# One load queue, a logarithm for the first two standard deviations, and moved copies in a fused attention and feed-forward kernel

## The chip, the cores and the metric

The kernel runs on one core of one Trainium2 chip. A core has five engines that run on their own and wait for each other by semaphores: TensorE (PE in the profile; its weight loads are listed apart as PEld), VectorE (DVE), ScalarE (ACT), GpSimd (POOL), and SyncE (SP), which here only issues DMA transfers. Each engine works through its own list of instructions in order: an instruction that waits holds up all behind it on the same engine, and nothing on the others unless they need its result. The metric is device time in microseconds (us); less is better. The median of three runs before the change is 281.26 us (281.19 to 281.33).

## What is computed

A transformer block on x of 2048 rows by 640 columns, in bf16: linear attention with 32 heads of 20 columns, then a gated feed-forward of width 1536. Cut to what matters:

```python
qkv = layernorm(x) @ wqkv                      # q, k, v per head, head width 20
pq, pk = q @ w_phi[h], k @ w_phi[h]
phi_q = concat(softmax(pq), softmax(-pq));  phi_k = concat(softmax(pk), softmax(-pk))
kv = sum_s phi_k[s] (x) v[s];  z = sum_s phi_k[s]
o  = (phi_q @ kv) / (phi_q . z + 1e-6)
h  = x + o @ wo
y  = layernorm(h)
out = h + (gelu(y @ w_gate) * (y @ w_up)) @ w_down
```

A layernorm here is (x - mean) / sqrt(var + 1e-5) with no weights. The q-by-w_phi and k-by-w_phi products are folded into the weights once: Wk2 = W_k times a block-diagonal of w_phi, likewise Wq2.

## The kernel before, in words

The 2048 rows are 16 tiles t = 0..15 of 128 rows, four tiles to a block b = 0..3 (`x_sb[b]`). The order of the work on every engine is the order of the program text (a manual schedule); no planner moves anything.

**Loads** (lines 160 to 178). The first row tile (`x_sb[0][:,0]`), tiles 2 and 3, then W_v in three pieces, tiles 4 and 5, W_k by a transposing DMA (`WkT`), tiles 8 to 11, W_q transposed (`WqT`), tiles 12 to 15 are issued from SyncE in that order; tile 1, `wphi` and tiles 6 and 7 are issued from ScalarE. ScalarE loads its table for `Exp` by a first small activation (line 168).

**Start** (lines 345 to 377). Ten matmuls on zeros keep TensorE busy. For each of tiles 0 to 3: `ln_st` takes the mean and variance with two `bn_stats` over 320 columns and one `bn_aggr` on VectorE (lines 106, 110), then 1/std on GpSimd by an addition and a power of -0.5 (lines 112, 114); `ln_ap` applies it on VectorE (line 130, tile `ln`); `ln_tp` transposes on TensorE into a PSUM tile `tp` (line 138) and copies it into `LN1T` (line 139). An argument `between` puts another operation after the first of the two `bn_stats`. `v_part` and `v_tile` are the products with W_v (`pv`), evacuated by ScalarE to `vS` (line 271). `BD`, the block-diagonal of w_phi, is one VectorE operation (line 356). `fold` (lines 201 to 226) forms W_k times BD in five pieces d = 0..4 (`wa`), each copied from PSUM by ScalarE for even d and by VectorE for odd d. PSUM tiles come from one pool of four double banks (`psG`), so a product can start only when the tile that used its bank has been evacuated.

**K loop** (lines 382 to 421), t = 0..15: product with Wk2 (`pk`), two `Exp` on ScalarE (`E`, line 283), V product and evacuation for tile t+4, layernorm applied for tile t+6 and transposed by DMA, row sums (`sk`, line 290), reciprocals and scaling of V (`vt`, line 298), and the accumulation `kvp`. At t = `T3` the PSUM pool is closed and reopened with three tiles and the accumulator. At t = 4..8 (`FQ`) one piece of W_q is folded.

**Q and attention for the first tiles** (lines 610 to 643): products with Wq2 (`pq`), two `Exp` each (`Eq`, line 343), and attention of tiles 0 and 1.

**Feed-forward** (lines 656 to 665). `weave(units, stages)` runs a list of units, `gate_up` (a gate and an up product, `gu`, then Gelu on ScalarE and a product on VectorE) and `down` (`pd`, 12 matmuls for each half of 640 columns), and puts each stage of a later tile's attention in front of the unit whose index it names; a stage whose index is past the last unit is kept for the next `weave`. The eight stages of a tile are `attn_a` (`ab`), `attn_b`, `attn_b2`, `attn_b3`, `attn_c` (product `po` with W_o), `attn_d` (VectorE: residual and row sum), `attn_d2` (ScalarE: squares; GpSimd: five small operations to 1/std) and `attn_e` (ScalarE: layernorm; DMA transpose into `LN2T`). With `SHORT2 = (0, 2, 3, 4, 10, 10, 11, 13)` and start index i, `attn_c` of the tile is at i + 10 and `attn_e` at i + 13. The second `weave` has 16 units: 12 `gate_up` for columns 256 to 511 of block 0, then four `down`. The third starts with `gate_up` of block 1, which reads `LN2T` of tiles 4 to 7 whole. The last `down` of the kernel is done in two halves, each added to the residual (`y`, line 575) and stored.

Of the kernel before, what the change touches and what calls it, by code (L numbers as in the profile page):

```python
# [9 lines left out]
F32 = mybir.dt.float32  # L10
# [7 lines left out]
def kernel(  # L18
# [12 lines left out]
    nc = tc.nc  # L31
# [12 lines left out]

    H0 = [(P * c) // Dh for c in range(NC)]
    NH = [(P * c + P - 1) // Dh - H0[c] + 1 for c in range(NC)]
    NWARM = 10
    VP = (0, 2, 4, 6, 9, 11)
    FQ = (4, 5, 6, 7, 8)

    QG = ((0, 1), (2, 3), (4, 5), (6,), (7, 8), (9, 10), (11, 12), (13, 14), (15,), (16, 17), (18, 19))
    QT = (15, 15, 15, 15)
    WA, WB = 2,0
    T3 = 3
    VC = Dh + 1
    KC = Dh + 2

# [26 lines left out]
    kmask = const.tile([P, NC, 4], BF16, name="kmask")  # L84
    BD = const.tile([P, NC, 8, Dh], BF16, name="BD")
    nhalf = const.tile([P, 2], F32, name="nhalf")

    def eq(t, c, s):
        for E, g in zip(Eq, QG):
# [6 lines left out]
    def gtile(name):  # L96
        return psG.tile([P, 2, 512], F32, name=name, tag="G")

    def ln_stats(pool, tiles, tag, act=True, between=None):

        n = len(tiles)
        mv = small(pool, [P, n, nc.vector.BN_AGGR_DIM], "mv" + tag)
        stats = small(pool, [P, n, 2, nc.vector.BN_STATS_DIM], "stats" + tag)
        for j, xt in enumerate(tiles):
            for i in range(2):
                nc.vector.bn_stats(stats[:, j, i, :], xt[:, i * HD:(i + 1) * HD])  # L106
                if between and i == j == 0:
                    between()
        for j in range(n):
            nc.vector.bn_aggr(mv[:, j, :], stats[:, j])  # L110
        ve = small(pool, [P, n], "ve" + tag)
        nc.gpsimd.tensor_scalar_add(ve, mv[:, :, 1], EPS)
        rstd = small(pool, [P, n], "rstd" + tag)
        nc.gpsimd.tensor_tensor(rstd, ve, nhalf[:, 0:n], op=ALU.pow)  # L114

        mr = small(pool, [P, n], "mr" + tag)
        if act:
            for j in range(n):
                nc.gpsimd.tensor_scalar(mr[:, j:j + 1], mv[:, j, 0:1], rstd[:, j:j + 1], -1.0,
                                        op0=ALU.mult, op1=ALU.mult)  # L120
        return [(xt, mv[:, j, 0:1], rstd[:, j:j + 1], mr[:, j:j + 1]) for j, xt in enumerate(tiles)]
# [11 lines left out]
    def transpose_to(dst, src, on_pe, on_dve=False):  # L133

        if on_pe:
            tp = psG.tile([P, 16, P], BF16, name="tp", tag="G")
            for c in range(NC):
                nc.tensor.transpose(tp[:, c, :], src[:, c * P:(c + 1) * P], ident)
            (nc.vector.tensor_copy if on_dve else nc.scalar.copy)(dst, tp[:, 0:NC, :])  # L139
        else:  # L140
            nc.sync.dma_start_transpose(dst, src)

# [15 lines left out]


    nc.gpsimd.memset(nhalf, -0.5)  # L160
    nc.sync.dma_start(x_sb[0][:, 0:1, :], x_v[:, 0:1, :])
    nc.scalar.dma_start(x_sb[0][:, 1:2, :], x_v[:, 1:2, :])
    nc.sync.dma_start(x_sb[0][:, 2:4, :], x_v[:, 2:4, :])
    for c0, c1 in ((0, 2), (2, 4), (4, 5)):
        nc.sync.dma_start(Wv[:, c0:c1, :], w_v[:, c0:c1, 2 * D:3 * D])

    ones = fp.tile([P, 2], F32, name="ones")
    nc.scalar.activation(ones, nhalf, ACTF.Exp)
    nc.scalar.dma_start(wphi, phi_v.rearrange("(c p) f -> p c f", p=P))
    nc.sync.dma_start(x_sb[1][:, 0:2, :], x_v[:, 4:6, :])  # L170
    nc.scalar.dma_start(x_sb[1][:, 2:4, :], x_v[:, 6:8, :])
    nc.sync.dma_start_transpose(WkT, A_wqkv[:, D:2 * D])
    wo_v = A_wo.rearrange("(c p) n -> p c n", p=P)
    wg_v = B_w_gate.rearrange("(c p) n -> p c n", p=P)
    wu_v = B_w_up.rearrange("(c p) n -> p c n", p=P)
# [25 lines left out]
    def fold(WT, W2, halves, ds=range(NC)):  # L201


        runs = []
        for c in range(NC):
            lo, hi = H0[c] * Dh, (H0[c] + NH[c]) * Dh
            for u in range(2):
                a, b = max(lo, u * HD), min(hi, (u + 1) * HD)
                if a < b:
                    runs.append((u, c, a, b))  # L210
        runs.sort()
        for d in ds:
            wa = gtile("wa")
            for i, (u, c, a, b) in enumerate(runs):
                nc.tensor.matmul(wa[:, u, a - u * HD:b - u * HD], lhsT=WT[:, c, d * P:(d + 1) * P],  # L215
                                 rhs=BD[:, c].rearrange("p a b -> p (a b)")[:, a - H0[c] * Dh:b - H0[c] * Dh],
                                 start=(i == 0 or runs[i - 1][0] != u),
                                 stop=(i + 1 == len(runs) or runs[i + 1][0] != u), skip_group_check=True)
            dst, src = W2[:, d, :].rearrange("p (u f) -> p u f", u=2), wa[:, :, 0:HD]
            if halves:  # L220
                dst = W2[:, d, :].rearrange("p (c u f) -> p u c f", c=NC, u=2)
                src = src.rearrange("p u (c f) -> p u c f", c=NC)
            if d % 2 == 0:
                nc.scalar.copy(dst, src)
            else:
                nc.vector.tensor_copy(dst, src)

    lnp, Ek, Vt = {}, {}, {}

    def ln_st(*tiles, act=True, between=None):  # L230
        for t, v in zip(tiles, ln_stats(p1, [x_sb[t // 4][:, t % 4, :] for t in tiles], "1", act, between)):
            lnp[t] = v

    def ln_ap(t, on_act=False, on_pe=False):
        ln = (ln_act if on_act else ln_dve)(p1, "1", *lnp[t])
        if on_pe:
            lnp[t] = ln
        else:
            transpose_to(LN1T[t // 4][:, :, t % 4 * P:(t % 4 + 1) * P], ln, False)

    def ln_tp(t, on_dve=False):
        transpose_to(LN1T[t // 4][:, :, t % 4 * P:(t % 4 + 1) * P], lnp[t], True, on_dve)
# [98 lines left out]
    def q_exp(j, signs=(0, 1)):  # L341
        for s in signs:
            nc.scalar.activation(Eq[j][:, :, s, :], pqs[j][:, 0:len(QG[j])], ACTF.Exp, scale=(1.0, -1.0)[s])  # L343

    ln_st(0, act=False)
    ln_st(1, act=False)
    ln_ap(0, on_pe=True)
    ln_tp(0)
    warm(WA)
    ln_st(2, act=False, between=lambda: ln_ap(1, on_pe=True))  # L350
    ln_tp(1)
    warm(WB)
    ln_st(3, act=False)
    ln_ap(2, on_pe=True)

    nc.vector.tensor_tensor(BD, wphi[:, :, None, :].to_broadcast([P, NC, 8, Dh]),
                            hmask[:, :, :, None].to_broadcast([P, NC, 8, Dh]), ALU.mult)
    ln_ap(3, on_pe=True)
    v_part(0, 0, 1, 2, 3, 4)
    v_part(1, 0, 1)  # L360
    ln_tp(2)
    v_part(1, 2, 3, 4)
    ln_tp(3)
    v_ev(0)
# [175 lines left out]
    def attn_ln(t, on_pe=False):  # L540
        st[t] = (ln_dve if on_pe else ln_act)(p2, "2", *st[t])
# [20 lines left out]
    def down(b, tl, u):  # L562
        if u == 0:
            st["pd"] = gtile("pd"), p2.tile([P, D], BF16, name="y", bufs=4)
        pd, y = st["pd"]
        if u == 1 and b == NB - 1 and tl == 3:
            pd = gtile("pd")
        for f in range(NF):
            nc.tensor.matmul(pd[:, u, 0:HD], lhsT=st[b, "g", f][:, tl * P:(tl + 1) * P],  # L569
                             rhs=Wd[:, f, u * HD:(u + 1) * HD],  # L570
                             start=(f == 0), stop=(f == NF - 1))
        last = b == NB - 1 and tl == 3
        if u == 1 or last:
            a = u if last else 0
            nc.vector.tensor_tensor(y.rearrange("p (u f) -> p u f", u=2)[:, a:u + 1], pd[:, a:u + 1, 0:HD],  # L575
                                    x_sb[b][:, tl, :].rearrange("p (u f) -> p u f", u=2)[:, a:u + 1], ALU.add)
            stores.append((lag, o_v[:, 4 * b + tl, a * HD:(u + 1) * HD], y[:, a * HD:(u + 1) * HD]))
            if b == NB - 1 and tl >= 2:
                store(lag)
# [23 lines left out]
    def gus(b, a0, a1):  # L603
        return [(gate_up, b, f, a0, a1) for f in range(NF)]
# [33 lines left out]
    attn_e(0, True, True)  # L638
    q_mm(q + 6)
    q_exp(q + 6)  # L640
    attn_ln(1, True)
    attn_e(1, True, True)
    attn_a(2, 2)
# [2 lines left out]
    def attn_at(t, i, offs):  # L646
# [9 lines left out]
    weave(gus(0, 0, 256) + downs(0, (0, 1)),  # L656
          attn_at(2, 0, (-1, 0, 1, 2, 7, 7, 8, 10)) + attn_at(3, 1, SHORT) + attn_at(4, 6, SHORT2) + attn_at(5, 9, SHORT2) +
          attn_at(6, 13, SHORT2))
    weave(gus(0, 256, 512) + downs(0, (2, 3)), attn_at(7, 1, SHORT2))
    for b in range(1, NB):  # L660
        stages = []
        if b + 1 < NB:
# [34 lines left out]
```

The softmax here doesn't subtract the row's maximum and nothing guards it: scores larger than these inputs give would overflow.

## Time and profile before

| What | Value |
|---|---|
| median of 3 runs | 281.26 us |
| span of the profiled execution | 279.4 us |
| TensorE busy | 271.9 us, 97% |
| VectorE, ScalarE, GpSimd busy | 166.0, 139.9, 96.5 us |
| granted TensorE clock | 1.00 |

The profile gives, for each engine, how long it was busy; then rows of instructions grouped by source line and operands; and the chain of work that ended last, followed back from the last instruction to what released it each time. A share of busy time is an average over stages with different limits: in the 10 us from 20 to 30 us VectorE is busy 9.75 us and ScalarE 8.79 us, in the 20 us from 240 to 260 us 6.55 and 5.58 us. A busy TensorE is not one at its peak, since the ends of pipelined matmuls are modelled.

### The profile page before, as it was taken

The page shows a single profiled execution, that of the slowest core. Times are in us where ns is not written, and L with a number is a line of the kernel's source. Part 1 is how long each engine was busy: PE and PEld are TensorE (multiplying, and loading weights), DVE is VectorE, ACT ScalarE, POOL GpSimd, SP SyncE. Part 2 cuts the span into 40 slices and gives each one's busy share as a digit, 9 for nine tenths or more (in the row PEclk, how much of TensorE's full clock was granted, in tenths as well). Part 3 has the DMA queues.
Part 4 walks back from the last instruction along what each step waited for, and adds up shares of the span by engine and source line. Part 5 has one row for each costly group of instructions (what it writes and reads, how often), then busy time and mean ns, then how long its engine had stood idle before and what let it go on. Part 6 is the DMA issues. An engine that isn't in the chain of part 4 may idle for free.

```text
span 279.4 us, 5750 instructions
## 1 busy us (share of the span) xinstructions
PE 271.9 (97%) x2326; PEld 171.5 (61%) x2326; DVE 166.0 (59%) x289; ACT 139.9 (50%) x226; POOL 96.5 (35%) x211
## 2 busy tenths in 40 slices
PE   5899999999999999999999999999999999999995
PEld 2676677774655788788764555675455567444573
DVE  5899998789396586676324848322667532333222
ACT  2589888758596847355434454413446340222200
POOL 5448986794302216453401243300135230000000
PEclk9999999999999999999999999999999999999999
DMA  7991323694440021322520103221031513000011
GB/s 231 265 260 25 55 49 46 176 396 158 142 145 0 2 45 29 70 50 68 52 70 2 36 20 66 42 77 47 2 47 23 74 23 94 26 1 0 0 49 47
DMA packets 40347, 21.05 MB, mean 75 GB/s; under 512 B 33152, under 2 KB 38400, under 8 KB 40320
## 3 DMA queue, kind: packets, MB, share of 16 engines
q1 hardware_dynamic: 39376, 20.16, 28.8%
q10 hardware_dynamic: 944, 0.52, 0.7%
q8 instruction: 18, 0.29, 0.5%
q14 instruction: 9, 0.07, 0.1%
HBM read 10.18 MB, written 2.62 MB: 46 GB/s over the span
## 4 chain that ended last, share of the span: by engine, by line
PE 89%; DVE 4%; ACT 3%; DMA 1%; POOL 1%; issue 1%; ACTq 0%
PE gu L554 37%; PE pd L569 19%; PE pq L338 8%; PE po L509 8%; PE pk L251 7%; PE pv L251 5%; PE ab L449 2%; PE kvp L316 2%; DVE stats L106 1%; DMA x_sb<-in_A_x_dram 1%; DVE sk L290 1%; ACT E L283 1%; POOL rstd L114 1%; ACT Eq L343 1%; PE wa L215 1%
## 5 line engine op out<-in xcount | busy, mean ns | idle before, releaser
L557 ACT ACTIVATE g<-gu 128x512 bf16<-128x512 f32 (+1 forms) x60 | 30.7, 512 | 76.1 <-PE gu L554 75.1
L560 DVE TENSOR_TENSOR GT<-gu,g 128x512 bf16<-128x512 f32 (+1 forms) x60 | 34.5, 581 | 53.6 <-ACT g L557 53.4
L554 PE MATMUL gu<-LN2T,Wg 128*128 128x512 bf16 (+1 forms) x300 | 61.9, 337 | 0.5 <-DVE GT L560 0.4
L554 PE MATMUL gu<-LN2T,Wu 128*128 128x512 bf16 (+1 forms) x300 | 61.7, 336 | 0.0
L569 PE MATMUL pd<-Wd,GT 128*128 128x320 bf16 x384 | 53.8, 299 | 0.0
L569 PEld LDWEIGHTS <-GT 128*128 128x128 bf16 x384 | 37.4, 98 | 15.7 <-DVE GT L560 0.9
L554 PEld LDWEIGHTS <-Wu 128*128 128x128 bf16 x300 | 29.4, 98 | 22.6
L554 PEld LDWEIGHTS <-Wg 128*128 128x128 bf16 x300 | 28.4, 98 | 21.3 <-issue 0.5
L251 PEld LDWEIGHTS <-LN1T 128*128 128x128 bf16 x300 | 28.5, 98 | 11.6 <-issue 0.7
L298 POOL TENSOR_TENSOR vt<-vS,rs 128x672 bf16<-128x672 bf16 x22 | 29.2, 1345 | 9.1 <-DVE rs L294 8.5
L575 DVE TENSOR_TENSOR y<-pd,x_sb 128x640 bf16<-128x640 f32 (+1 forms) x17 | 13.3, 784 | 30.6 <-PE pd L569 30.6
L457 ACT COPY AB<-ab 128x704 f32<-128x704 f32 x28 | 19.5, 748 | 13.7 <-PE ab L449 13.5
L290 DVE TENSOR_REDUCE sk<-E 128x64 f32<-128x1280 bf16 x16 | 23.3, 1455 | 3.4 <-ACT E L283 3.4
L490 DVE TENSOR_TENSOR tt<-AB,w 128x1280 bf16<-128x1280 f32 x16 | 23.8, 1486 | 2.1 <-POOL w L483 2.0
L251 PE MATMUL pk<-Wk,LN1T 128*128 128x320 bf16 x160 | 24.1, 299 | 0.4 <-ACT E L283 0.3
L509 PE MATMUL po<-Wo,oT 128*128 128x320 bf16 x160 | 24.4, 299 | 0.0
L283 ACT ACTIVATE E<-pk 128x640 bf16<-128x640 f32 x32 | 20.8, 705 | 6.9 <-PE pk L251 6.7
L338 PE MATMUL pq<-LN1T,Wq 128*128 128x512 bf16 x100 | 22.9, 379 | 0.0
L251 PE MATMUL pv<-Wv,LN1T 128*128 128x320 bf16 x140 | 21.3, 299 | 0.0
L343 ACT ACTIVATE Eq<-pq 128x1024 bf16<-128x1024 f32 (+1 forms) x22 | 19.4, 950 | 3.7 <-PE pq L338 3.7
L509 PEld LDWEIGHTS <-oT 128*128 128x128 bf16 x160 | 15.6, 98 | 7.2 <-ACT oT L139 0.2
L125 ACT ACTIVATE ln<-x_sb,v,rstd 128x640 bf16<-128x640 bf16 x14 | 12.9, 919 | 10.5 <-POOL v L537 10.3
(80 smaller groups left out, 258.8 us busy)
## 6 DMA issues: line engine op xcount, KB each, us to landing
out_dram<-y SPq DMA_DIRECT2D x15, 160.0 KB, 1.8
Wg<-in_B_w_gate_dram SPq DMA_DIRECT2D x1, 1920.0 KB, 7.6
Wu<-in_B_w_up_dram SPq DMA_DIRECT2D x1, 1920.0 KB, 15.1
Wd<-in_B_w_down_dram SPq DMA_DIRECT2D x1, 1920.0 KB, 8.0
x_sb<-in_A_x_dram SPq DMA_DIRECT2D x2, 640.0 KB, 4.7
Wo<-in_A_wo_dram SPq DMA_DIRECT2D x1, 800.0 KB, 9.3
x_sb<-in_A_x_dram SPq DMA_DIRECT2D x2, 320.0 KB, 4.8
Wv<-in_A_wqkv_dram SPq DMA_DIRECT2D x2, 320.0 KB, 6.2
```

The source lines that it names most:

```text
L251: nc.tensor.matmul(ps[:, u, 0:HD], lhsT=lnT(t, c), rhs=W[:, c, u * HD:(u + 1) * HD], start=(c == 0), stop=(c == NC - 1))
L283: nc.scalar.activation(Ek[t][:, s, :].rearrange("p (u f) -> p u f", u=2), pk[:, :, 0:HD], ACTF.Exp, scale=(1.0 if s == 0 else -1.0))
L290: nc.vector.reduce_sum(sk, Ek[t].rearrange("p s (h f) -> p (s h) f", f=Dh), axis=AX.X)
L298: eng.tensor_tensor(vt[:, s], vS[t % 6], rs[:, s * H:(s + 1) * H, None].to_broadcast([P, H, VC]), ALU.mult)
L338: nc.tensor.matmul(pqs[j][:, i, :], lhsT=Wq2[:, kc, c * P:(c + 1) * P], rhs=LN1T[b][:, kc, :], start=(kc == 0), stop=(kc == NC - 1))
L343: nc.scalar.activation(Eq[j][:, :, s, :], pqs[j][:, 0:len(QG[j])], ACTF.Exp, scale=(1.0, -1.0)[s])
L490: nc.vector.tensor_tensor(tt.rearrange("p s (h f) -> p s h f", f=Dh), num, w[:, :, :, None].to_broadcast([P, 2, H, Dh]), ALU.mult)
L509: nc.tensor.matmul(po[:, u, 0:HD], lhsT=st[t][:, c, :], rhs=Wo[:, c, u * HD:(u + 1) * HD], start=(c == 0), stop=(c == NC - 1))
L554: nc.tensor.matmul(gu[:, i, 0:n], lhsT=W[:, c, f * P:(f + 1) * P], rhs=LN2T[b][:, c, a0:a1], start=(c == 0), stop=(c == NC - 1))
L557: nc.scalar.activation(g[:, 0:n], gu[:, 0, 0:n], ACTF.Gelu_apprx_tanh)
L560: nc.vector.tensor_tensor(st[b, "g", f][:, a0:a1], gu[:, 1, 0:n], g[:, 0:n], ALU.mult)
L569: nc.tensor.matmul(pd[:, u, 0:HD], lhsT=st[b, "g", f][:, tl * P:(tl + 1) * P], rhs=Wd[:, f, u * HD:(u + 1) * HD], start=(f == 0), stop=(f ...
```

## The change

It puts all first loads on SyncE's queue in the order in which they are used, with W_k ahead of tiles 6 and 7; takes 1/std of tiles 0 and 1 as exp(-0.5 ln(var + eps)) on ScalarE, from one table that has both functions; splits the first transposed copy between ScalarE and VectorE; reorders the operations of tiles 0 to 3 and starts the V product of tile 0 earlier; gives ScalarE four of five W_k copies and all W_q copies; closes the first PSUM pool one iteration later; loads the Gelu table by a dummy activation after the last `Exp`; starts the attention of tile 7 two units later; and cuts the last half of the output in pieces of 192 and 128 columns, to shorten the work after the last matmul.

```diff
-    NWARM = 10
+    NWARM = 11
+    KA, QA = (0,1,2,4), (0,1,2,3,4)
-    WA, WB = 2,0
-    T3 = 3
+    WA = 1
+    T3 = 4
...
-        nc.gpsimd.tensor_scalar_add(ve, mv[:, :, 1], EPS)
-        nc.gpsimd.tensor_tensor(rstd, ve, nhalf[:, 0:n], op=ALU.pow)
+        if log:
+            nc.scalar.activation(ve, mv[:, :, 1], ACTF.Ln, bias=eps)
+            nc.scalar.activation(rstd, ve, ACTF.Exp, scale=-0.5)
+        else:
+            nc.gpsimd.tensor_scalar_add(ve, mv[:, :, 1], EPS)
+            nc.gpsimd.tensor_tensor(rstd, ve, nhalf[:, 0:n], op=ALU.pow)
...
+            if on_dve is None:
+                nc.scalar.copy(dst[:, 0:2, :], tp[:, 0:2, :])
+                nc.vector.tensor_copy(dst[:, 2:NC, :], tp[:, 2:NC, :])
...
     nc.sync.dma_start(x_sb[0][:, 0:1, :], x_v[:, 0:1, :])
-    nc.scalar.dma_start(x_sb[0][:, 1:2, :], x_v[:, 1:2, :])
+    nc.sync.dma_start(x_sb[0][:, 1:2, :], x_v[:, 1:2, :])
+    nc.scalar.add_instruction(mybir.InstLoadActFuncSet(name=nc.get_next_instruction_name(), act_func_set_id=6))
+    nc.sync.dma_start(Wv[:, 0:2, :], w_v[:, 0:2, 2 * D:3 * D])
+    nc.sync.dma_start(Wv[:, 2:4, :], w_v[:, 2:4, 2 * D:3 * D])
     nc.sync.dma_start(x_sb[0][:, 2:4, :], x_v[:, 2:4, :])
-    for c0, c1 in ((0, 2), (2, 4), (4, 5)):
-        nc.sync.dma_start(Wv[:, c0:c1, :], w_v[:, c0:c1, 2 * D:3 * D])
-    nc.scalar.activation(ones, nhalf, ACTF.Exp)
-    nc.scalar.dma_start(wphi, phi_v.rearrange("(c p) f -> p c f", p=P))
+    nc.sync.dma_start(Wv[:, 4:5, :], w_v[:, 4:5, 2 * D:3 * D])
+    nc.sync.dma_start(wphi, phi_v.rearrange("(c p) f -> p c f", p=P))
     nc.sync.dma_start(x_sb[1][:, 0:2, :], x_v[:, 4:6, :])
-    nc.scalar.dma_start(x_sb[1][:, 2:4, :], x_v[:, 6:8, :])
     nc.sync.dma_start_transpose(WkT, A_wqkv[:, D:2 * D])
+    nc.sync.dma_start(x_sb[1][:, 2:4, :], x_v[:, 6:8, :])
...
-            if d % 2 == 0:
+            if d in (QA if halves else KA):
                 nc.scalar.copy(dst, src)
...
-    ln_st(0, act=False)
-    ln_st(1, act=False)
-    ln_ap(0, on_pe=True)
-    ln_tp(0)
+    ln_st(0, act=False, log=True)
+    ln_st(1, act=False, between=lambda: ln_ap(0, on_pe=True), log=True)
+    ln_tp(0, None)
     warm(WA)
+    v_part(0, 0, 1, 2)
     ln_st(2, act=False, between=lambda: ln_ap(1, on_pe=True))
     ln_tp(1)
-    warm(WB)
-    ln_st(3, act=False)
-    ln_ap(2, on_pe=True)
+    v_part(0, 3, 4)
+    v_part(1, 0, 1)
+    ln_st(3, act=False, between=lambda: ln_ap(2, on_pe=True))
+    ln_tp(2)
+    ln_ap(3, on_pe=True)
     nc.vector.tensor_tensor(BD, ...)
-    ln_ap(3, on_pe=True)
-    v_part(0, 0, 1, 2, 3, 4)
-    v_part(1, 0, 1)
-    ln_tp(2)
     v_part(1, 2, 3, 4)
     ln_tp(3)
...
+        cuts = [(0, 192), (192, HD)] if last and u == 1 else [(0, HD)]
+        for n0, n1 in cuts:
+            ...   # matmuls, residual and store of columns n0 to n1
...
     q_exp(q + 6)
+    dummy = small(p2, [P, 2], "dummy", 1)
+    nc.scalar.activation(dummy, nhalf, ACTF.Gelu_apprx_tanh)
...
-    weave(gus(0, 256, 512) + downs(0, (2, 3)), attn_at(7, 1, SHORT2))
+    weave(gus(0, 256, 512) + downs(0, (2, 3)), attn_at(7, 3, SHORT2))
```

More of the change, by code (lines that the diff above doesn't have):

```diff
@@ L86 @@
     nhalf = const.tile([P, 2], F32, name="nhalf")
+    eps = const.tile([P, 1], F32, name="eps")
     def eq(t, c, s):
@@ L97, in gtile, with ln_stats @@
         return psG.tile([P, 2, 512], F32, name=name, tag="G")
-    def ln_stats(pool, tiles, tag, act=True, between=None):
+    def ln_stats(pool, tiles, tag, act=True, between=None, log=False):
         n = len(tiles)
@@ L138, in transpose_to @@
                 nc.tensor.transpose(tp[:, c, :], src[:, c * P:(c + 1) * P], ident)
-            (nc.vector.tensor_copy if on_dve else nc.scalar.copy)(dst, tp[:, 0:NC, :])
+            if on_dve is None:
+                nc.scalar.copy(dst[:, 0:2, :], tp[:, 0:2, :])
+                nc.vector.tensor_copy(dst[:, 2:NC, :], tp[:, 2:NC, :])
+            else:
+                (nc.vector.tensor_copy if on_dve else nc.scalar.copy)(dst, tp[:, 0:NC, :])
         else:
@@ L160 @@
     nc.gpsimd.memset(nhalf, -0.5)
+    nc.gpsimd.memset(eps, EPS)
     nc.sync.dma_start(x_sb[0][:, 0:1, :], x_v[:, 0:1, :])
-    nc.scalar.dma_start(x_sb[0][:, 1:2, :], x_v[:, 1:2, :])
+    nc.sync.dma_start(x_sb[0][:, 1:2, :], x_v[:, 1:2, :])
+    nc.scalar.add_instruction(mybir.InstLoadActFuncSet(name=nc.get_next_instruction_name(), act_func_set_id=6))
+    nc.sync.dma_start(Wv[:, 0:2, :], w_v[:, 0:2, 2 * D:3 * D])
+    nc.sync.dma_start(Wv[:, 2:4, :], w_v[:, 2:4, 2 * D:3 * D])
     nc.sync.dma_start(x_sb[0][:, 2:4, :], x_v[:, 2:4, :])
-    for c0, c1 in ((0, 2), (2, 4), (4, 5)):
-        nc.sync.dma_start(Wv[:, c0:c1, :], w_v[:, c0:c1, 2 * D:3 * D])
-    ones = fp.tile([P, 2], F32, name="ones")
-    nc.scalar.activation(ones, nhalf, ACTF.Exp)
-    nc.scalar.dma_start(wphi, phi_v.rearrange("(c p) f -> p c f", p=P))
+    nc.sync.dma_start(Wv[:, 4:5, :], w_v[:, 4:5, 2 * D:3 * D])
+    nc.sync.dma_start(wphi, phi_v.rearrange("(c p) f -> p c f", p=P))
     nc.sync.dma_start(x_sb[1][:, 0:2, :], x_v[:, 4:6, :])
-    nc.scalar.dma_start(x_sb[1][:, 2:4, :], x_v[:, 6:8, :])
     nc.sync.dma_start_transpose(WkT, A_wqkv[:, D:2 * D])
+    nc.sync.dma_start(x_sb[1][:, 2:4, :], x_v[:, 6:8, :])
     wo_v = A_wo.rearrange("(c p) n -> p c n", p=P)
@@ L228, with ln_st @@
     lnp, Ek, Vt = {}, {}, {}
-    def ln_st(*tiles, act=True, between=None):
-        for t, v in zip(tiles, ln_stats(p1, [x_sb[t // 4][:, t % 4, :] for t in tiles], "1", act, between)):
+    def ln_st(*tiles, act=True, between=None, log=False):
+        for t, v in zip(tiles, ln_stats(p1, [x_sb[t // 4][:, t % 4, :] for t in tiles], "1", act, between, log)):
             lnp[t] = v
@@ L567, in down @@
             pd = gtile("pd")
[L568 to L571, printed above, removed]
         last = b == NB - 1 and tl == 3
[L573 to L579, printed above, removed]
+        cuts = [(0, 192), (192, HD)] if last and u == 1 else [(0, HD)]
+        for n0, n1 in cuts:
+            if n0:
+                pd = gtile("pd")
+            for f in range(NF):
+                nc.tensor.matmul(pd[:, u, n0:n1], lhsT=st[b, "g", f][:, tl * P:(tl + 1) * P],
+                                 rhs=Wd[:, f, u * HD + n0:u * HD + n1], start=(f == 0), stop=(f == NF - 1))
+            if u == 1 or last:
+                a = u if last else 0
+                r = lambda x: x.rearrange("p (u f) -> p u f", u=2)[:, a:u + 1, n0:n1]
+                nc.vector.tensor_tensor(r(y), pd[:, a:u + 1, n0:n1], r(x_sb[b][:, tl, :]), ALU.add)
+                f0, f1 = a * HD + n0, u * HD + n1
+                stores.append((lag, o_v[:, 4 * b + tl, f0:f1], y[:, f0:f1]))
+                if b == NB - 1 and tl >= 2:
+                    store(lag)
     later, stores, lag = [], [], 3
```

## The prediction

> **What bounds the kernel now.** I read the chain of waits first, cut by time, then the order of instructions on each engine where the chain leaves TensorE.
>
> From the chain, in order of time (start us, us, what), the first part of the start:
>
> ```profile
> 6.17 0.42 POOL ve L112
> 6.67 0.57 POOL rstd L114
> 7.26 0.45 DVE ln L130
> ...
> 9.44 0.23 POOL ve L112
> 9.74 1.42 POOL rstd L114
> 11.18 0.46 DVE ln L130
> 11.68 0.45 PE tp L138 x5
> ...
> 16.21 0.60 ACT Wk L224
> 16.86 1.57 PE pk L251 x10
> ...
> 21.46 1.31 ACT E L283 x2
> 22.79 1.50 DVE sk L290
> ...
> 31.61 1.52 PE pk L251 x10
> ```
>
> Up to 11.68 us the layernorm of tiles 0 to 3 sets the end, through VectorE and GpSimd. The first K product then waits for a W_k copy until 16.86, and from 21.46 to 31.61 ScalarE and VectorE carry the chain. From there it is TensorE without a gap until 91.6, and again from 95.77 to 276.46. So time can come only from before 31.6, from the 4 us around 91.6 to 95.8, and from the 2.9 us after the last matmul; whatever makes TensorE wait in between is added whole.
>
> The break at 91.6, in the timeline (start, duration, engine, line, operation):
>
> ```profile
> 91.62 1.94 ACT L343 ACTIVATE Eq<-pq 128x1024 bf16<-128x1024 f32 x2 [0.50 <-PE pq L338]
> 93.58 1.28 ACT L557 ACT_TABLE_LOAD   x1
> 94.88 0.38 ACT L557 ACTIVATE g<-gu 128x256 bf16<-128x256 f32 x1
> 95.29 0.42 DVE L560 TENSOR_TENSOR GT<-gu,g 128x256 bf16<-128x256 f32 x1 [1.20 <-ACT g L557]
> 95.77 0.71 PE L554 MATMUL gu<-LN2T,Wg 128*128 128x256 bf16 x5 [0.37 <-DVE GT L560]
> ```
>
> The table load begins 0.02 us after the last Exp: it does not wait for the gate product. The last Exp itself waited for TensorE.
>
> The layernorm chain of one feed-forward tile (tile 6), undisturbed, in the timeline:
>
> ```profile
> 131.34 0.81 DVE L523 SCALAR_TENSOR_TENSOR x_sb<-po,x_sb 128x640 bf16<-128x640 f32 x1
> 132.20 0.74 ACT L530 ACTIVATE sq<-x_sb 128x640 bf16<-128x640 bf16 x1 [0.38 <-DVE x_sb L523]
> 133.21 0.27 POOL L534 TENSOR_SCALAR v<-sm,v 128x1 f32<-128x1 f32 x1 [0.36 <-ACT sq L530]
> 134.53 0.92 ACT L125 ACTIVATE ln<-x_sb,v,rstd 128x640 bf16<-128x640 bf16 x1 [0.46 <-POOL v L537]
> ```
>
> **What the Trainium skill says.** "ScalarE: Activation LUTs", section "What ACT_TABLE_LOAD costs", prices an activation with immediates at 186 ns plus 0.83 ns an element, a pointer operand at 93 ns more, and a table load at 1283 ns; the trace agrees (0.20 us for the 128x2 Exp at 2.52, 1.28 us for both loads). "SBUF — State Buffer", section "Who interferes with whom", says that a VectorE tensor_tensor with both inputs in SBUF shuts out a GpSimd operation that reads SBUF; the trace agrees: the power at 9.74 took 1.41 us beside the BD product (0.97 us from 9.75), 0.57 us otherwise. "DMA: Bandwidth & Descriptors", section "Issuing engines are not separate DMA queues", says that SP's and ACT's transfers run on the same 16 engines and interleave. So one queue moves no more bytes, it only orders them.
>
> **The change part by part.**
>
> *1/std of tiles 0 and 1.* Before, from the end of `bn_aggr` (5.09) to the layernorm of tile 0 (6.10) is 1.01 us. After: a handoff of 0.04, Ln with a pointer bias 0.28, Exp 0.19, 0.05 of gaps, hence 5.65: 0.45 us earlier. The Exp and Ln tables come as one load, in place of the old one. What is queued behind on ScalarE is the copy of the first two chunks of `LN1T`, which now waits for tile 1's Exp (about 7.2); the V product starts near 7.6 (8.06 before).
>
> *Loads.* Tiles 2 and 3 landed at 5.05 (issue 1.25, 3.8 to land) and now stand behind 640 KB of W_v. In stretches of 1 us the DMA moved 15, 230, 397, 276, 350, 350 KB from 1 to 7 us; the 1280 KB up to their end are through near 6.05. Transfers landed 0.7 us (tile 0: 320 KB through at 3.2, landed 3.93) to 1.6 us (first W_v piece) after their bytes by the same count: 6.75 to 7.65; I take 7.2. VectorE would want them at 7.0 (aggregate of tile 1 to 6.7, then its part of the copy, 0.35 us by the 0.48 us of a whole one). That is 0.2 us of wait, with all VectorE work behind it. Tile 0 alone in front may land up to 0.3 us earlier; this is lost at the same wait, so I count nothing. W_k is issued at about 4.1 (4.5 before), and its landing at 12.7 already came before the fold at 14.0: nothing. Tiles 6 and 7 are issued at some 10.3, behind W_k. Half-way between its 12.7 and the 15.2 at which the 640 KB behind it landed is 14.0; VectorE wants them near 14.9, so hidden.
>
> *Order of tiles 2 and 3.* With tile 2 at 7.2: first half 7.65, layernorm 1 to 8.07, second half 8.49, aggregate 8.73, GpSimd 0.09 + 0.23 + 0.09 + 0.57 to 9.71, layernorm 2 to 10.2. Now the second half of tile 3 stands *behind* layernorm 2: 10.6, aggregate 10.8, GpSimd 11.77 (no BD beside it, so 0.57 and not 1.41), layernorm 3 to 12.25, transpose at 12.3. Before: 11.68. **+0.6 us** (0.4 if tile 2 is there in time, 1.0 at 7.65). The V matmuls moved ahead of it end near 11.3 and wait for it all the same.
>
> *W_k copies.* Before, ScalarE's W_k piece 0 ends at 15.24, it idles 0.28, and copies `vS` from 15.52 and piece 2 until 16.81, which the first K product waits for. Piece 1 now goes between: 0.60 more (0.70 with 0.1 overlapped), less most of the idle time and counting handoffs: **+0.25 us**. VectorE loses 0.82 us of work there, but would only wait for the next E. The shift passes through 21.46 to 31.61, where VectorE and ScalarE follow that product.
>
> *W_q copies, T3.* Two of 0.76 us leave VectorE and come to ScalarE as 0.70 each, at about 35 and 42 us. From 31 to 46 us ScalarE is busy 12.9 of 15 and TensorE has no gap: nothing gained, 0 to 0.3 lost; I take 0. The fourth PSUM tile for one iteration longer touches only stage t = 3, where TensorE waited 0.24 us for a DMA and not for a bank: 0.
>
> *Dummy Gelu.* The table load already ran without waiting. Added is one small activation, 0.19 us less 0.1 overlapped, ahead of the Gelu whose product releases TensorE: **+0.1** (to 0.2).
>
> *Tile 7.* Start 3 puts `attn_c` at unit 13 and `attn_e` at index 16, past the last of 16 units, hence ahead of the first unit of the next weave, which reads its result. From the end of `po` TensorE has three `down` units, 36 x 0.136 = 4.89 us, `ab` 0.50 and 0.1 of changeover: 5.5 us. The chain needs, from tile 6 above: 0.06, then 131.34 to 135.45 (4.11), 0.02, and 2.6 us for a transposing DMA into `LN2T` to land: 6.8 us. Nothing else is queued on ScalarE or ahead on SP. **+1.3 us** of TensorE wait, nothing behind it to hide it. Before, four `down` and a `gate_up` gave 8.0 us. The stages that move within gapless TensorE work cost nothing. Nor do the changed counts of matmuls on zeros: all run while TensorE waits for `ln` or `LN1T`.
>
> *Tail.* 12 matmuls more but the same columns: 0. The last residual has 128 columns in place of 320: 0.49 falls to 0.29 by the line through 0.82 (640) and 0.49 (320): **-0.2**. The store's 1.6 us to land stay.
>
> Sum: 0.6 + 0.25 + 0.1 + 1.3 - 0.2 = +2.05: **283.3 us**.
>
> **Rivals.**
> - *The start gains, tile 7 loses.* Loads land early enough, and the 0.45 us carry through: 281.26 - 0.45 + 0.1 + 1.3 - 0.2 = 282.0. For it: the lag of landings is uncertain by 0.9. Against: the second GpSimd round trip of tile 3 now follows layernorm 2.
> - *The start loses, tile 7 is hidden* by some slack I did not see: 281.26 + 0.85 + 0.1 - 0.2 = 282.0. Against: the stage indices are exact.
> - *Faster.* The start gains 0.45 and 0.25 of tile 0's landing, VectorE relieved of two copies' worth gains 0.3 in the 20 to 31 us chain, tile 7 hidden, tail 0.2: 281.26 - 1.2 = 280.1. For it: VectorE is busy 9.75 of 10 us there; against: the removed copies lie outside it.
> - *Worse.* ScalarE becomes the bound of the K loop (+0.3), or tiles 6 and 7 come late and hold VectorE (+0.5): 284.1.
>
> **How the numbers follow.** Forecast 0.55, then 0.15, 0.10, 0.12, 0.08. The middle two scatter about 282.0, a third of them under 281.8. Slower 0.55 + 0.08 + 0.17 = 0.80, same 0.08, faster 0.12. The range leaves out the faster case and part of the worst: 281.8 to 284.0.
>
> **What would show it.** The changed profile should have a TensorE wait of about 1.3 us at the first `gu` of block 1, released by the DMA into `LN2T`; the transpose of tile 3 later than 11.68 with tile 2's `bn_stats` waiting for its load; the first `pk` near 17.7, after a W_k copy; the table load still right behind the last Exp, a small Gelu after it; and a last residual near 0.29 us. I am wrong if `gu` starts there without a wait, or if the first `pk` comes before 16.9.

## The result and the profile after

Measured side by side, the changed kernel takes **284.16 us** (median of four, 284.08 to 284.21) and the kernel before 281.29 us: ratio 1.0098, 95% interval 1.008 to 1.0115. It is slower by about 2.9 us. The direction was as predicted; the time lies 0.9 us above the 283.3 and 0.16 us above the upper end of the range.

The chain of waits of the changed kernel, in order of time (start us, us, what), over the stretch that was shown for the kernel before:

```profile
4.34 0.30 ACT ve L117
4.67 0.21 ACT rstd L118
4.91 0.45 DVE ln L137
...
6.36 0.20 ACT rstd L118
6.56 0.27 ACT LN1T L148
6.85 0.36 DVE LN1T L149
7.21 0.41 DVE stats L108
...
9.62 0.45 DVE ln L137
10.07 0.41 DVE stats L108
...
11.19 0.57 POOL rstd L121
11.78 0.46 DVE ln L137
12.29 0.47 PE tp L145 x5
...
17.05 0.60 ACT Wk L237
17.69 1.57 PE pk L264 x10
...
31.23 3.46 DMA LN1T<-ln
...
41.98 4.11 DMA LN1T<-ln
```

Tile 0's layernorm starts at 4.91 in place of 6.10, and yet tile 3's transpose comes at 12.29 in place of 11.68. From 9.62 on the order is layernorm 2, statistics of tile 3, GpSimd, layernorm 3, one behind the other. The first K product follows a W_k copy, at 17.69 in place of 16.86. The last two lines are new: two transposing DMAs into `LN1T` are on the chain inside the K loop, which ran "TensorE without a gap" before. That loop was not quite without a wait: in the kernel before one weight load waited for a transpose,

```profile
26.77 2.56 PEld L251 LDWEIGHTS <-LN1T 128*128 128x128 bf16 x20 [0.24 <-DMA LN1T<-ln]
```

which is the 0.24 us that the prediction names under `T3`.

The stretch around the table load in the changed kernel, in the timeline (start, duration, engine, line, operation, idle time before it and what ended that):

```profile
93.33 1.94 ACT L356 ACTIVATE Eq<-pq 128x1024 bf16<-128x1024 f32 x2 [0.50 <-PE pq L351]
95.29 1.28 ACT L660 ACT_TABLE_LOAD   x1
96.58 0.20 ACT L660 ACTIVATE dummy<-nhalf 128x2 f32<-128x2 f32 x1
96.69 0.37 ACT L569 ACTIVATE g<-gu 128x256 bf16<-128x256 f32 x1
97.09 0.42 DVE L572 TENSOR_TENSOR GT<-gu,g 128x256 bf16<-128x256 f32 x1 [1.29 <-ACT g L569]
97.57 0.71 PE L566 MATMUL gu<-LN2T,Wg 128*128 128x256 bf16 x5 [0.46 <-DVE GT L572]
```

The load stands behind the last `Exp` as before, and the dummy adds 0.09 us to TensorE's wait (0.46 for 0.37). This wait is 0.46 or 0.47 in all eleven profiles of kernels with the dummy and 0.37 in all seven without it.

Tile 7 in the timeline of the changed kernel:

```profile
140.60 0.82 DVE L535 SCALAR_TENSOR_TENSOR x_sb<-po,x_sb 128x640 bf16<-128x640 f32 x1 [1.85 <-PE po L521]
...
143.78 0.92 ACT L132 ACTIVATE ln<-x_sb,v,rstd 128x640 bf16<-128x640 bf16 x1 [1.48 <-POOL v L549]
144.72 1.20 SPq L153 DMA_TRANSPOSE LN2T<-ln  x1
145.39 0.57 PE L461 MATMUL ab<-KV,Eq 64*128 64x88 bf16 x20
...
147.34 1.25 PE L566 MATMUL gu<-LN2T,Wg 128*128 128x512 bf16 x5 [1.38 <-DMA LN2T<-ln]
```

TensorE waits 1.38 us for the transpose of tile 7. The last residual takes 0.29 us in place of 0.49.

Where the 3.1 us between the two profiled spans (279.4 and 282.5) lie, from the start times of the first product of each stage:

| Stretch | before | after | difference | predicted |
|---|---|---|---|---|
| span's start to first `pk` | 16.86 | 17.69 | +0.83 | +0.85 |
| first `pk` to first `pq` (K loop) | 45.50 | 46.38 | +0.88 | 0 |
| dummy (`gu` wait for `GT`) | 0.37 | 0.46 | +0.09 | +0.1 |
| first `gu` of block 1 | 144.07 | 147.34 | +3.27, less the three above +1.47 | +1.3 |
| last residual | 0.49 | 0.29 | -0.20 | -0.2 |

So the question for the experiments is the K loop, and whether the start's 0.83 is what the kernel does or what one execution did.

### The profile page after: what moved, and what is told of

Read it like the earlier page. It is cut to its first block, busy times and chain, and to the rows that moved or that the text cites. A ratio compares the mean times of both kernels' runs of the same rounds, so it can differ in the third digit from the quotient of the medians.

```text
span 282.5 us, 5785 instructions
## 1 busy us (share of the span) xinstructions
PE 273.1 (97%) x2338; PEld 171.9 (61%) x2338; DVE 164.2 (58%) x288; ACT 141.9 (50%) x233; POOL 94.9 (34%) x208
## 4 chain that ended last, share of the span: by engine, by line
PE 83%; ACT 5%; DVE 5%; DMA 4%; issue 1%; POOL 1%; ACTq 0%; POOLq 0%
PE gu L566 36%; PE pd L587 17%; PE pq L351 8%; PE po L521 8%; PE pk L264 6%; PE pv L264 3%; DMA LN1T<-ln 3%; PE ab L461 2%; PE kvp L329 2%; DVE stats L108 1%; ACT vS L284 1%; DVE sk L303 1%; DMA LN2T<-ln 1%; DMA x_sb<-in_A_x_dram 1%; ACT Eq L356 1%
## 5 line engine op out<-in xcount | busy, mean ns | idle before, releaser
L587 PE MATMUL pd<-Wd,GT 128*128 128x320 bf16 (+2 forms) x396 | 54.0, 295 | 0.0
L587 PEld LDWEIGHTS <-GT 128*128 128x128 bf16 x396 | 38.0, 98 | 15.4 <-DVE GT L572 0.9
L311 POOL TENSOR_TENSOR vt<-vS,rs 128x672 bf16<-128x672 bf16 x22 | 29.8, 1372 | 10.5 <-DVE rs L307 9.1
L592 DVE TENSOR_TENSOR y<-pd,x_sb 128x640 bf16<-128x640 f32 (+3 forms) x18 | 13.5, 750 | 28.7 <-PE pd L587 28.7
```

What stands on the lines that cost most here:

```text
L311: eng.tensor_tensor(vt[:, s], vS[t % 6], rs[:, s * H:(s + 1) * H, None].to_broadcast([P, H, VC]), ALU.mult)
L587: nc.tensor.matmul(pd[:, u, n0:n1], lhsT=st[b, "g", f][:, tl * P:(tl + 1) * P], rhs=Wd[:, f, u * HD + n0:u * HD + n1], start=(f == 0), sto ...
```

## The experiments

Ratios are to the kernel before, on the same chip in the same session; the bracket is the 95% interval. Each run has one profile, of one of its executions, and where that was the fastest or slowest of the run it is said. Runs are named e1 to h4.

**The K loop: the transposes' source rows.** The new constant `eps` has a slot of its own and moves the tiles that are allocated after it by 32 bytes. The layernorm's source rows for the DMA transposes into `LN1T` began at multiples of 256 bytes in the built program; now they begin 32 bytes past one. The landing of a transpose into `LN1T` is 2.6 us (median of ten) in place of 2.4.

```diff
-    nhalf = const.tile([P, 2], F32, name="nhalf")
-    eps = const.tile([P, 1], F32, name="eps")
+    nhalf3 = const.tile([P, 3], F32, name="nhalf")
+    nhalf, eps = nhalf3[:, 0:2], nhalf3[:, 2:3]
```

> The changed kernel with eps as a third column of nhalf, so that no new tile moves the tiles behind it: the source rows of the transposes into LN1T lie on multiples of 256 bytes again. Theory A (the address of the source rows makes these transposes slow): landings go back from 2.6 to about 2.4 us, the waits of TensorE for LN1T (0.46 and 0.32 us) go, and the time falls by 0.5 to 0.9 us, to 283.3 to 283.7. Rival C (all loads on one queue, or the W_q copies on ScalarE, make them slow or late): landings stay at 2.6 us and the time at 284.2.

Measured (e1) 1.0085 (1.0069 to 1.0101): landings back at 2.4 us, K loop 45.55 us, first `pk` at 18.12. In this profile the loop's 0.88 us are gone, but the start is later, and the ratio's interval overlaps that of the change; the median, 283.94 us, stays above the 283.3 to 283.7 of theory A.

Two unused constants in the kernel *before*, of 32 and 64 bytes, do the same from the other side:

```diff
+    pad = const.tile([P, 8], F32, name="pad")     # 16 columns in the second kernel
+    nc.gpsimd.memset(pad, 0.0)
```

> The kernel before with one unused tile of 32 bytes in front of the tiles of the first pool, nothing else. Theory A (source rows off a multiple of 256 bytes) and theory B (off a multiple of 64 bytes): transposes into LN1T land in 2.6 us and more, TensorE waits for tile 9, time up by 0.3 to 0.9, to 281.6 to 282.2. Rival C: no change, 281.3.

Measured (e3) 0.999 (0.9979 to 1.0000); landings 2.6 us, K loop 45.46: the landings of theory A, without its cost.

> The same with 64 bytes: the source rows lie on a multiple of 64 but not of 256 bytes. Theory A: as with 32 bytes, 281.6 to 282.2. Theory B: as the kernel before, 281.3, landings 2.4 us. Rival C: no change, 281.3.

Measured (e4) 1.0002 (0.9991 to 1.0013); landings 2.6 us too, so a multiple of 64 bytes is not enough. In its profiled execution, the slowest of 14 (282.41 us), the K loop took 45.99 us, with 1.0 us of weight loads waiting for transposes: the kernel before has the long loop too at times. Slower transposes alone cost it nothing that its median shows.

The changed kernel was therefore profiled twice more, and the aligned one once more.

> The changed kernel once more, unchanged, for a second trace and more timed runs on the chip of the next three. Theory J (the K loop's extra 0.9 us is partly chance: an instruction fetch falls on the transposes of tiles 9 and 12, and how long these then take differs between executions): the stretch from the first K product to the first Q product differs from 46.4 us by 0.3 us or more, and the time from the earlier 1.0098 of before. Theory S (all of it is in the program): 46.4 us again.

> The changed kernel once more, unaltered, as the partner of the other three. Theory (start and K loop vary from execution to execution): ratio 1.009 to 1.010, first K product anywhere from 17.7 to 19.1, K loop (first K product to first Q product) 45.5 to 46.4. Rival (the 46.4 of its first profile is what the kernel does): K loop 46.3 to 46.5 again.

> The kernel of e1 once more (the new eps column inside nhalf, so that the layernorm's source rows lie on multiples of 256 bytes again), beside h3 on the same chip. Theory (the slower transposes cost the K loop part of its 0.9 us): K loop at 45.5 and 0.2 to 0.8 us less than h3 in the median. Rival (the transposes have slack, the K loop varies by itself): K loop anywhere from 45.5 to 46.4, medians within 0.2 us.

Measured: 1.0099 (1.0085 to 1.0114) for the second execution (f1), 1.0092 (1.0077 to 1.0108) for the third (h3) and, aligned again (h4), 1.0075 (1.0059 to 1.0092). The waits for `LN1T` between 16 and 66 us, in the view of waits (engine and line, what it waited for: us in total, times, longest; PEld and PE wait side by side, so the two are not added), for four executions, first the changed kernel:

```profile
PEld L264 <- DMA LN1T<-ln: 1.4, 3, 0.6
PE pv L264 <- DMA LN1T<-ln: 0.5, 1, 0.5
```

the same kernel in its second execution (f1):

```profile
PEld L264 <- DMA LN1T<-ln: 0.5, 1, 0.5
```

aligned, first execution (e1):

```profile
PEld L264 <- DMA LN1T<-ln: 0.2, 1, 0.2
```

and aligned, second execution (h4):

```profile
PEld L264 <- DMA LN1T<-ln: 0.9, 3, 0.4
PE pv L264 <- DMA LN1T<-ln: 0.2, 1, 0.2
```

Their K loops took 46.38, 45.49, 45.55 and 46.02 us (46.05 in h3): the loop follows these waits. The long waits come from single late transposes (up to 4.1 us to land), in aligned kernels too. The transfer view of the changed kernel from 31 to 35.5 us shows one (40 slices; busy tenths, then GB/s; below, the transfers of one instruction queue: number, MB, share of the engines):

```profile
DMA  0000000000051899999900000084000000000200
GB/s 0 0 0 0 0 0 0 0 0 0 0 146 34 180 216 216 214 191 84 16 7 9 11 9 9 9 177 74 0 0 0 0 0 0 0 0 0 73 0 0
q8 instruction: 1, 0.02, 1.3%
```

From the fourteenth slice it moves at 180 to 216 GB/s for five slices of 0.11 us, falls off, and trickles at 7 to 16 GB/s for seven more, until a last burst. The 146 GB/s at the beginning are the one transfer of the instruction queue q8 (16 KB, from 32.24 to 33.19 us).

The packets of all 18 traces show that the late transposes are no accident of one execution. Of the ten transposes into `LN1T`, those of tiles 9 and 12 meet such a 16 KB transfer of q8 in every trace: it overlaps the movement of their data or ends less than 0.1 us before it, in 36 of 36 cases, and their data then take 1.2 to 2.3 us to move. Those of tiles 7, 8, 10, 11, 13 and 14 meet none, in 108 cases, and take 0.83 to 0.84 us in aligned kernels and 0.94 to 0.96 in the others (one took 1.12). The further the instruction transfer reaches into the transpose, the longer it takes: 0.4 to 0.6 us more where it ended within 0.3 us of the first data, 1.0 to 1.45 more where it ended 0.8 us or more after. Where it falls differs between executions of the same kernel: it ended 0.78 and 1.28 us into the two transposes in the changed kernel's first profile, and 0.17 and 0.60 in its second. No run moved these transfers, so this is a regularity of the traces and not an experiment.

So two things go with a longer transpose: the shifted rows, by about 0.1 us of movement and 0.2 of landing in every one, and the instruction transfers, by up to 1.4 us in two or three of ten. By the traces, the second decides the length of the loop in one execution. What the first is worth in the changed kernel is not settled: the medians of h3 and h4, from one session, lie 0.51 us apart (284.31 and 283.80), as the theory of h4 had it, but their intervals overlap, and the loop of h4 was not short, in a profile of its slowest execution of six (284.57).

**Tile 7**, undone in the changed kernel and done alone in the kernel before:

```diff
-    weave(gus(0, 256, 512) + downs(0, (2, 3)), attn_at(7, 3, SHORT2))
+    weave(gus(0, 256, 512) + downs(0, (2, 3)), attn_at(7, 1, SHORT2))
```

> The changed kernel with the attention of tile 7 back at start index 1. If the stage past the last unit is what costs, the wait of 1.4 us at the first gate product of block 1 goes whole and the time falls by 1.4, to 282.8. If the wait is only moved (to another LN2T, or to a bank of PSUM), it falls by less than 0.7.

> The kernel before with the attention of tile 7 started at index 3 instead of 1, nothing else. By the prediction's step TensorE waits 1.3 to 1.4 us at the first gate product of block 1 for the DMA into LN2T, and the time rises by as much, to a ratio of 1.0047 to 1.005. Rival: it needs the changed kernel's other edits, ratio 1.000 to 1.002.

Undone (e2): 1.0029 (1.0021 to 1.0037), no wait for `LN2T`. Alone in the kernel before (f2): 1.0056 (1.0043 to 1.007), that is 1.6 us (1.2 to 2.0), with the same wait in its timeline:

```profile
145.12 1.25 PE L554 MATMUL gu<-LN2T,Wg 128*128 128x512 bf16 x4 [1.37 <-DMA LN2T<-ln]
```

This part is settled: the edit costs a wait of 1.4 us in either kernel, and 1.6 of the 2.9 us of loss when done alone.

**The order of tile 3's statistics**, both halves ahead of layernorm 2, as before:

```diff
-    ln_st(3, act=False, between=lambda: ln_ap(2, on_pe=True))
+    ln_st(3, act=False)
+    ln_ap(2, on_pe=True)
```

> The changed kernel with both halves of tile 3's statistics ahead of layernorm 2 on VectorE, as in the kernel before. If the second half behind layernorm 2 is what makes tile 3 late, its transpose comes near 11.2 us (12.3 in the changed kernel), the first K product 0.8 to 1.1 us earlier, and the time falls by as much. Rival: the copies on ScalarE or the loads bind first, and the first K product stays within 0.3 us of 17.7.

Measured (f3) 1.006 (1.0048 to 1.0072), 1.0 us below the unaltered changed kernel of the same session (282.73 and 283.73 us); the transpose of tile 3 at 11.35, the first `pk` at 16.76, as early as in the kernel before. The two GpSimd round trips in a row are thus the cost of the new order at the start.

**The first loads.** In the second execution of the changed kernel (f1; the slowest of its five, 284.76 us) the first `pk` came at 19.11, 1.4 us later than in the first. VectorE's timeline there:

```profile
5.78 0.21 DVE L112 BATCH_NORM_AGGREGATE mv<-stats 128x2 f32<-128x12 f32 x1
6.84 0.36 DVE L149 COPY LN1T<-tp 128x384 bf16<-128x384 bf16 x1 [0.85 <-ACT LN1T L148]
8.54 0.49 DVE L108 BATCH_NORM_STATS2 stats<-x_sb 128x6 f32<-128x320 bf16 x1 [1.34 <-DMA x_sb<-in_A_x_dram]
```

Tiles 2 and 3 landed at 8.5 us here and at 7.1 in the first execution; in the third (h3) at 7.3. In the four profiles with the load order of before (before, e3, e4, f2) they landed at 4.85 to 5.15. Two kernels move the loads, first tiles 2 and 3 ahead of W_v on the one queue, then all loads back to the two queues of before (only the table load stays):

```diff
+    nc.sync.dma_start(x_sb[0][:, 2:4, :], x_v[:, 2:4, :])
     nc.sync.dma_start(Wv[:, 0:2, :], w_v[:, 0:2, 2 * D:3 * D])
     nc.sync.dma_start(Wv[:, 2:4, :], w_v[:, 2:4, 2 * D:3 * D])
-    nc.sync.dma_start(x_sb[0][:, 2:4, :], x_v[:, 2:4, :])
```

> The changed kernel with the load of x tiles 2 and 3 alone moved ahead of both pieces of W_v. Theory (the load order costs, by how late it lands): tiles 2 and 3 land near 5 us in every run, the first K product comes at 17.4 to 17.7 without the 18.1 and 19.1 of other runs, ratio 1.004 to 1.008 against 1.0099. Rival: the chain through VectorE and GpSimd alone sets the start (two round trips in a row), landing at 7.1 is early enough: ratio 1.009 to 1.010.

> The changed kernel with the first loads on two queues in the order of before (the table load stays). Theory A (the one queue gains on tile 0 and loses on tiles 2 and 3): tile 0 lands 0.85 us later (its bn_stats at 3.96 in place of 3.1), which the chain of VectorE passes on up to tile 2, so that the first K product comes 0.3 to 0.8 us later than the 17.7 of the changed kernel: ratio 1.010 to 1.012. Theory B (the late tiles 2 and 3 are the larger cost): the first K product at 17.3 to 17.7 and no execution late: ratio 1.006 to 1.008.

With tiles 2 and 3 ahead (g3): 1.0073 (1.006 to 1.0086), the first `pk` at 17.68 and no wait for the load, but the second W_v piece is waited for instead, by 0.19 us. Its median is 0.40 us below that of g4, an otherwise nearly unaltered changed kernel in the same session. With two queues (h1): 1.0100 (1.0085 to 1.0115), the median 0.15 us above that of h3, `bn_stats` of tile 0 at 3.88 in place of 3.13 (h3), the transpose of tile 3 at 13.06 in place of 12.51, the first `pk` at 18.46 in place of 17.92. So the one queue as a whole is not what costs: it brings tile 0 earlier by 0.8 us, which the start needs. What costs in some executions is the place of tiles 2 and 3 behind W_v.

**1/std by Ln and Exp**, undone:

```diff
-    ln_st(0, act=False, log=True)
-    ln_st(1, act=False, between=lambda: ln_ap(0, on_pe=True), log=True)
+    ln_st(0, act=False)
+    ln_st(1, act=False, between=lambda: ln_ap(0, on_pe=True))
```

> The changed kernel with 1/std of tiles 0 and 1 by GpSimd's power, as before, in place of Ln and Exp on ScalarE. Theory (what Ln and Exp gain is lost at the bn_stats of tile 2, which stands behind the VectorE part of the copy and the late load): ln of tile 0 0.3 us later, the transpose of tile 3 at 12.3 to 12.6, ratio as the changed kernel or up to 0.001 above. Rival: the 0.34 us of tile 0 and as much of tile 1 come through: transpose of tile 3 at 12.9, ratio 1.012.

Measured (h2) 1.0085 (1.0069 to 1.0102), 284.00 us beside 284.31 of h3. Layernorm 0 starts at 5.31 in place of 4.92 (h3), but the transpose of tile 3 at 12.65 in place of 12.51. The 0.39 us that the logarithm gains are used up before tile 3.

**The copies**, divided as before (`KA`, `QA` = (0, 2, 4)):

```diff
-    KA, QA = (0,1,2,4), (0,1,2,3,4)
+    KA, QA = (0,2,4), (0,2,4)
```

> The changed kernel with the block-diagonal copies divided between ScalarE and VectorE as in the kernel before (KA and QA = (0, 2, 4)). Prediction's terms: the W_k copies cost 0.25 us, the W_q copies nothing, so the first K product comes 0.2 to 0.25 us sooner after the transpose of tile 3 (5.15 to 5.2 in place of 5.4), ratio 1.009. Rival: with ScalarE the bound of the K loop the two W_q copies cost up to 0.9 us as well: K loop 45.5 in place of 46.4, ratio 1.006.

Measured (g4) 1.0085 (1.0069 to 1.01). From the transpose of tile 3 to the first `pk` 5.18 us in place of 5.40: the W_k copies cost 0.22. The K loop took 46.13 us with the W_q copies back on VectorE, with 1.0 us of weight loads waiting for `LN1T`: in this profile the loop is long without them, so the W_q copies are not what lengthened it.

**All together.** One kernel keeps the one queue, the early V product and the cut tail, and undoes the rest: aligned `eps`, tile 7 at 1, copies as before, no dummy, `T3` = 3, whole first copy on VectorE, both halves of tile 3's statistics in one, and takes 1/std of all four tiles by Ln and Exp. Two more set `T3` = 4, one of them with tiles 2 and 3 loaded ahead of W_v.

```diff
-    ln_st(2, act=False, between=lambda: ln_ap(1, on_pe=True))
+    ln_ap(1, on_pe=True)
     ln_tp(1)
+    ln_st(2, act=False, log=True)
...
-    ln_st(3, act=False, between=lambda: ln_ap(2, on_pe=True))
+    ln_st(3, act=False, log=True)
+    ln_ap(2, on_pe=True)
```

> What the traces point to: the changed kernel's loads and its tail; 1/std by Ln and Exp for tiles 0 to 3; the first transposed copy whole on VectorE; both halves of tile 3's statistics ahead of layernorm 2; eps in the spare column of nhalf; tile 7 at index 1; W_k and W_q copies, T3 and the Gelu table as in the kernel before. If the start is set by that chain, the transpose of tile 3 comes near 10.4 us (11.7 before), the first K product near 15.6 (16.9 before), and with 0.2 us at the tail the time is 1.2 to 1.5 us below before, a ratio of 0.9947 to 0.9957. Rival: the K loop, bound by VectorE, or tiles 6 and 7 landing near 13.6, take back what the start gains: ratio 0.998 to 1.000.

> The combined kernel of f4 with T3 = 4 alone, so that the fourth PSUM tile stays with the K loop one stage longer. Theory: the wait of the K product of tile 3 for the vS evacuation (0.86 us) goes, and the K loop shortens by about 0.5 (46.0 to 45.5): ratio 0.997 to 0.999. Rival: ScalarE and VectorE hold the loop there and the wait only moves: ratio 1.000, K loop 46.0.

> The combined kernel of f4 with T3 = 4 and the load of x tiles 2 and 3 moved ahead of both pieces of W_v on the one queue. If the load order makes the start late (theory), tiles 2 and 3 land near 5 us in place of 7.1 to 8.5, VectorE never waits for them, and the first K product comes at 15.5 to 15.9; with the bank free, the 0.86 us before the K product of tile 3 go: ratio 0.996 to 0.998 of the kernel before (280.3 to 280.8 us). Rival: VectorE and GpSimd set the start and something else takes the place of the bank wait: ratio 0.999 to 1.000.

With `T3` = 3 (f4): 0.9999 (0.999 to 1.0009); the 1.2 to 1.5 us that were expected did not come. In its profiled execution, the fastest of 13 (280.54 us), the first `pk` came at 15.88, 1 us ahead of the kernel before, and most of it was given back at once:

```profile
25.46 1.52 PE L264 MATMUL pk<-Wk,LN1T 128*128 128x320 bf16 x10 [0.86 <-ACT vS L284]
```

With `T3` = 4 (g2): **0.9978** (0.9969 to 0.9988), the best of all, faster than both kernels. The wait of 0.86 us is gone, yet its K loop is 45.96 us beside 46.01, and the medians of the two kernels (281.18 and 281.19 us) come from different sessions; what `T3` is worth is not settled. Its profiled execution waited 0.86 us for tiles 2 and 3 and began `pk` at 16.69. With those loaded first (g1): 0.9986 (0.9977 to 0.9996). There, in the slowest execution of 22 (282.40 us), the first `pk` came at 17.40 and not at the expected 15.5 to 15.9: the first V product waited for W_v until 7.83 (6.47 in g2), and VectorE waited 0.61 us for tiles 6 and 7, so the load that comes last only changed its name. None of these three tells how much each part undone brought.

## Why the prediction was right or wrong

- **What bounds the kernel:** right as far as it went. The loss lies before the first `pk`, in the K loop and at tile 7, and whatever made TensorE wait was added whole.
- **Tile 7, +1.3:** right in mechanism and nearly in size: 1.38 us of wait, 1.47 in the stretch, 1.6 (1.2 to 2.0) alone. Undersized by 0.1 to 0.3.
- **Order of tiles 2 and 3, +0.6:** the named cause, the second half of tile 3's statistics behind layernorm 2, is shown by f3, where undoing it gave 1.0 us. That the transpose of tile 3 came +0.61 in the first execution, as reckoned, is in part luck. Tile 2's statistics were to wait for their load; they waited for VectorE's part of the split copy, and began at 7.21 all the same, because tile 0 landed 0.85 us earlier than before while that copy stood 0.85 us behind ScalarE's part. Without the early tile 0, in h1, the transpose comes at 13.06.
- **W_k copies, +0.25; dummy, +0.1; tail, -0.2:** right: 0.22, 0.09 and 0.20.
- **1/std, gained and lost again:** right, by h2. The way differed: the gain went not only into the late load but into that wait of 0.85 us, since ScalarE's part of the copy stands behind tile 1's Exp.
- **Loads:** landing was taken as 7.2, within 6.75 to 7.65. In the first execution it was 7.1, but 8.5 in the second: **the range of this term was too narrow**, and four of the eleven profiles with this load order lie above it (7.7 to 8.5). That tile 0 would land at most 0.3 us earlier was wrong too (0.85), and only the copy hid it. Tiles 6 and 7 were hidden as predicted: no wait for them in the changed kernel. What the prediction took from the Trainium skill, "DMA: Bandwidth & Descriptors", section "Issuing engines are not separate DMA queues", that transfers of both issuing engines interleave, agrees with the traces: with one queue tile 0 is in use 0.8 us earlier, and tiles 2 and 3 land 2.0 to 3.6 us later, at 7.1 to 8.5 in place of 4.85 to 5.15.
- **"W_q copies, T3 ... I take 0": this is the step that failed.** The copies themselves cost nothing (g4), but this term stood for the whole K loop. It took "TensorE has no gap" for slack in the transposes, although the 0.24 us of waiting for a DMA at t = 3, which it names itself, is a weight load waiting for a transpose. The slack was small: the transpose of tile 9 cost no wait where it landed 2.9 us after its issue (before, f1), and 0.4 to 0.6 us of weight loads where it took 3.2 to 3.5 (the changed kernel's first profile, h3, h4, e4). The loop grew by 0.88 us in the first profile, most of the 1.05 us by which that profile's difference exceeded the forecast (3.1 against 2.05). Waits for `LN1T` grew with it, and the two transposes on its chain, at 31.23 and 41.98, are those of tiles 9 and 12, which met a transfer of the instruction queue. I had also not seen that `eps` moves the source rows. The Trainium skill, "DMA: Bandwidth & Descriptors", section "How a descriptor splits into AXI transactions", says that when a descriptor does not start at a multiple of 256 bytes, its first transaction starts at the multiple below and the bytes in front still cost; 2.6 us for 2.4 agrees with it.

One profile is not the median. Over the ten profiles of the changed kernel that keep its order of tiles 2 and 3 (itself three times; e1, e2, g3, g4, h1, h2 and h4 with one other edit each), the first `pk` comes at 18.13 us on average and the K loop takes 45.89 (18.24 and 45.97 in the three unaltered ones); over the four of the kernel before (itself, e3, e4, f2) 17.01 and 45.59. By these the start costs 1.1 us in place of 0.85, the K loop 0.3 in place of 0, tile 7 about 1.5 in place of 1.3: with dummy and tail 2.8 us, against 2.87 between the medians. So three undersizings, all to the same side, make the miss, and the K loop is the one that was put at nothing. Its 0.3 us is no more than the scatter (45.49 to 46.38 in the ten, 45.42 to 45.99 in the four), and how much of it the change causes stays open.

The range ended at 284.0 because the case "worse" (284.1) was put partly outside. The cost of that case came, though not by its causes: neither ScalarE as the bound of the K loop nor tiles 6 and 7. The two rivals at 282.0 and the faster one are refuted by the first `pk` after 16.9 and by the wait at tile 7. Part of the faster one is real: with the order of tile 3 mended and tile 7 put back, g2 is faster by 0.22%. Its start gains in two of the three combined profiles (15.88 and 16.69, but 17.40 in g1, against 16.55 to 17.62 in the kernel before).

## What to carry to other kernels

A stage without a gap on the bounding engine is not a stage with slack: before adding a constant or shifting an order there, look at how long before its use each transfer lands, in the worst of its repetitions and not in the median, and at the instruction queues' transfers beside it. When loads are put in one queue, the one put last takes all the scatter, so ask which engine has its whole list behind it. A stage index that pushes the last link of a chain past the end of its list costs the whole chain less what is left to run, and this can be added up from rows of the profile. Where a stage varies between executions, one profile against one profile gives a wrong split of the loss: the K loop was 0.88 us by the first pair, 0.3 by fourteen profiles.

## What the runs showed of the hardware that was not expected

- A DMA transpose of 128x640 bf16 into `LN1T` lands in 2.4 us (medians) from source rows at multiples of 256 bytes, in 2.6 us from rows shifted by 32 or by 64 bytes; its data move in 0.83 to 0.84 us and in 0.94 to 0.96. The transposes of the same size into `LN2T`, whose source rows begin 128 bytes past a multiple in the built program of the kernel before, land in 2.6 us there too.
- A DMA transpose that meets a 16 KB transfer of the instruction queue takes 1.2 to 2.3 us to move its data (tiles 9 and 12 in all 18 traces), in aligned and shifted kernels; part of it then trickles at 7 to 16 GB/s after most moved at 180 to 216 GB/s.
- With all first loads on one queue the first tile of 160 KB was in use at 3.02 to 3.37 us, and at 3.69 to 4.14 us with two queues.
- The same kernel's first K product varied from 17.69 to 19.11 us over three executions, by the landing of one load (7.1 to 8.5 us).
